# Another explicit order for the parts of the first stage of a three-stage kernel on one core

## The chip, the cores and the metric

One core of one Trainium2 chip runs the whole kernel. The metric is device time in microseconds (us) of one execution; lower is better. Times are given as the median of three timed runs, and one further execution was recorded by the hardware profiler. In the rows, PE is TensorE's matmul queue and PEld its weight loads, DVE is VectorE, ACT is ScalarE, POOL is GpSimd and SP is SyncE, which here only issues DMAs. A letter q behind an engine's name means its sequencer, which waits, branches and issues DMAs while the engine stays idle. TensorE's clock has two levels in the rows, 2.4 and 1.2 GHz; the granted clock is given as a share of 2.4 GHz.

## What is computed

Three layers follow each other. The inputs are float32, and only the output of the last layer leaves the chip.

```python
def _attn_ref(x, state):                      # x: 4 x 8 x 512 x 64, state: 4 x 8 x 32 x 64
    scores = scale * np.matmul(x, state.transpose(0, 1, 3, 2))
    a = softmax(scores)                       # over the 32 states
    xread = np.matmul(a, state)
    scores2 = scale * np.matmul(state, x.transpose(0, 1, 3, 2))
    a2 = softmax(scores2)                     # over the 512 tokens
    sread = np.matmul(a2, x)
    return np.concatenate([xread, sread], axis=2)

def _moe_ref(x, w_gate, w1, w2, capacity):    # 2176 rows of 512, 8 experts, top 1
    logits = x @ w_gate
    expert_idx = np.argmax(logits, axis=1)
    # each row goes to its expert, in order, while the expert has room
    h = np.maximum(np.einsum('ecd,edf->ecf', disp, w1), 0.0)
    y = np.einsum('ecf,efd->ecd', h, w2)
    out[i] = gate_w[i] * y[expert_idx[i], pos[i]]

def _moe2_ref(x, w_in, w_out):
    h = x @ w_in
    return (h * np.clip(h + 3.0, 0.0, 6.0) / 6.0) @ w_out
```

## The kernel before, in words

The kernel is one function `full` with three stages. The first stage is `phase1`: attention for the four batches, the gate logits, the choice of an expert for each row, the place of each row in its expert's list, and the tables from which the second stage reads its trips. Towards its end the first expert tile (256 rows) is worked too. The second stage goes through the other expert tiles, and the third multiplies all rows with `w_in` and `w_out`.

**What sets the order.** `phase1` is written as some 150 named parts, most of them Python generators with a `yield` after an instruction or a few. The string `ORDER` lists the parts' names; each word runs its part to its next `yield` (`name*3` three times), and the tile framework is told to keep that order. So `ORDER` is a hand-written interleaving: an engine gets its instructions in the order in which the words make them, and executes its queue strictly in that order. A second constant, `ALT`, says which engine does some of the parts' operations.

```python
        going = {}
        for n, k in ((w.split("*") + [1])[0:2] for w in ORDER.split()):
            for _ in range(int(k)):
                if n not in going:
                    f, *a = parts.pop(n)
                    going[n] = f(*a) or iter(())
                next(going[n], None)
```

**The parts**, with batch b and half f (four heads each) as digits, `soft_max10` being batch 1, half 0:
- `tr` transposes the input tiles on TensorE (L276) and ScalarE copies them out (L278); `scores` multiplies (L284) into the PSUM tile `pss`. `soft_max` takes the row maximum from `pss` on VectorE (L294), `soft_exp` the exponential from `pss` on ScalarE (L300), and `turn` transposes `pss` in blocks on VectorE (L303). So `pss` is read by two engines.
- `read_max` reduces on VectorE (L311) and subtracts on GpSimd (L313, two operands in SBUF); `read_exp` is on ScalarE (L316); `read_sum` reduces on VectorE (L320 to L324) and multiplies on GpSimd (L326, two operands in SBUF) or, where `ALT` says so, on VectorE; `read_turn` is VectorE's (L329).
- `e2_turn` (L337, L339), `s_read` (L354), `s_scale` (L360 and four DMAs, L364), `s_turn` (L369, L372) and `s_logits` (L378, L380, L383 and a DMA, L386) make the 32 state rows of a batch and their logits. `read` with a batch and an index 0 to 7 multiplies (L400) and copies out (L403 VectorE, L405 ScalarE). `rows_out` (L409) stores the batch's rows to `x_rows` in DRAM (L412).
- `count` (L419 to L434), `total` (L439, L441), `first_expert` (L446 to L471), `sums` (L477, L478), `place` (L485 to L507), `before` (L513 to L517) and `lists` (L532 to L538) are chains of small VectorE instructions with some on GpSimd and ScalarE; `lists2` multiplies one-hot tiles (L544) and adds them to the list of rows `LT` (L547 for batch 0, L549 for the others). `tables` and `halves` (L665 to L781) make the trip tables on VectorE.
- `raws` loads the first expert's weights; `w00` to `w13` split each of the eight pieces into two parts: a cast on ScalarE (L824) and a subtraction of two SBUF operands (L826) on VectorE or GpSimd.
- `early` stores an empty row to `x_rows` by DMA (L617), and GpSimd writes into the source tile behind it (L618). `e_rows` casts the first row numbers (L951) and gathers 256 rows on GpSimd's queue (L858); `e_x` transposes them (L846, L849, L851), `e_m` is the first product of the first expert tile (96 matmuls at L903, L907, L909), `e_y` the second (96 matmuls at L921, L931), with the result stored at L937.

One PSUM tile, `bank`, holds many of the small results (`s_read`, `s_turn`, `s_logits`, `sums`, `lists2` and others write parts of it, and ScalarE and VectorE read them).

**Behind the first stage** GpSimd reads the table (L1347), casts row numbers from `LT` (L1133) and gathers the next tiles' rows (L858), TensorE transposes them (L846), and SP issues, in this order, the store of the first tile's result (L937), two loads of second-layer weights (L1080, L1082) and the next expert's weights (L814).

Of the kernel before, what the change touches and what calls it, by code (L numbers as in the profile page):

```python
# [32 lines left out]
    tr11 setup2*2 tr10 setup1 tr11 setup2 soft_exp01 read_max01 prep_gate e2_turn00 scores10 read_sum00 consts tr12 e2_turn00 s_read00 setup2  # L33
    e2_turn01 tr12 read_sum00*2 tr13 s_read00 setup2 soft_max10 read_max01 e2_turn01 tr13 s_read00 scores11 turn10 read_exp01 read_sum00 soft_exp10
    tr20 read_max10 inputs setup2 tr20 setup2 read_turn00 setup2*2 setup3 setup2 read_init0 read_sum01*2 soft_max11 read_sum01 read_init1 s_read01
    setup2 s_scale0 read06 read04 read_max10 turn11 read_exp10 soft_exp11 s_scale0 read_max11 tr21 tr22 tr21 read_sum01 scores20 setup3 tr23 s_read10
    read_sum10 setup3 s_read10 consts setup2 tr22 read04 read_sum10 e2_turn10 read_sum10 tr23 setup3 read_turn01 read_max11 read00 read_sum10 read06
    s_turn0 setup3 scores21 soft_max20 read_exp11 turn20 s_ids0 read05 read_turn10 read00 read_max20 turn21 read05 setup3 s_turn0 setup3 read_max20
    read_sum11 read01 read07 read01 read02 e2_turn10 read07 read03 soft_max21 s_logits0 read02 read03 read_exp20 read_max21 rows_out0 s_logits0 early
    read_sum11 count0 rows_out0 read_sum20 count0 e2_turn11 read10*2 count0 s_logits0 tr30 read_sum20 setup3 s_read10 e2_turn11 read_max21 count0 tr31  # L40
    setup3 s_scale0 setup3 read_sum11 setup3 count0 consts before0 setup3 tr30 read14 read_sum11 first_expert soft_exp20 read_exp21 first_expert tr31
    read_sum20 consts before0 read12 first_expert s_scale1 e2_turn20 read_sum21 first_expert*2 scores30 read_turn11 first_expert setup3 count0
    s_read11 setup3 first_expert before0 read_sum21 soft_exp21 s_read20 tr32 first_expert read_sum21 read15 read14 first_expert*2 raws total0 read12
    s_scale1 e2_turn20 tr32 soft_max30 s_read20 sums0 read13 place0 raws place0 e2_turn21 turn30 place0 read_sum21 read_turn21 s_turn1 read_sum20
    read13 tr33 place0 read_max30 raws read15 first_expert place0 e2_turn21 read16 read_turn20 place0 tr33 total0 place0 raws read_max30 place0
    s_read20 soft_exp30 s_scale2 read_init2 read11 scores31 s_logits0 s_turn1 place0 read17 lists0 e2_turn30 s_read21 read11 lists0 read16 read17 w00
    read27 lists0 s_logits1 s_scale1 read_exp30 lists0 read24 lists0 read27 read25 lists0 rows_out1 s_scale2 turn31 soft_max31 lists0*2 s_ids2
    soft_exp31 s_logits1 read_max31 s_turn2 read26 read25 lists0 count1 lists0*3 read24 first_expert lists20 count1 read26 read_sum30 consts read23
    lists20 s_read30 count1 read_max31 read20 e_rows read_exp31 read_sum30 s_read30 e2_turn31 s_turn2 read23 e2_turn30 count1 read20 e_rows read_sum30
    read21 e2_turn31 count1 read_sum31 rows_out1 before1 read_sum30 s_read30 s_logits2 read_sum31 count1 w01 read_turn30 consts read22 read_init3  # L50
    read22 read34 read_sum31 w02 read21 read32 read_sum31 read32 s_ids1 read30 read34 s_logits2 total1 read_turn31 w00 s_read31 sums1 e_x0 w03 read31
    read30 w02 read33 s_scale3 read31 e_x0 read36 e_x1 e_x0 s_scale3 e_ok before1 s_turn3 place1 read35 read33 rows_out2 total1 read37 raws count2
    before1 count2 e_g s_turn3 w01 e_x1 s_logits1 read36 w03 s_logits1 e_x1 read37 s_logits3 read35 s_logits3 place1 count2 rows_out3 e_m0 count2
# [1570 lines left out]
```

## Time and profile before

| | us |
|---|---|
| median of three runs | 563.12 |
| lowest and highest | 562.98, 563.13 |
| the profiled execution, as timed | 564.15 |
| span of the profiled execution, first instruction to last | 562.4 |

The profiled execution is 1.0 us above the median, and 1.75 us of its time lie outside its span. In the profile, the timeline lists an engine's instructions with start, duration and, in square brackets, the idle time ahead of an instruction and what ended it; neighbours of one line are merged (x2). The table of stretches gives for each stretch the busy time of each engine in us and its instructions (x), TensorE's granted clock as a share, the DMA engines' share and their rate. The chain of work goes back from the last instruction, at each step to what released it.

### The profile page before, as it was taken

To read this page: it belongs to the slowest core of one execution; us is meant where nothing else is said; L and a number is where in the kernel's file an instruction comes from. 1 tells how busy PE (TensorE), PEld (TensorE's weight loads), DVE (VectorE), ACT (ScalarE), POOL (GpSimd) and SP (SyncE) were. 2 spreads that over 40 slices of the span, in tenths; PEclk is the share of its full clock that TensorE was granted. 3 is DMA by queue.
4 is the path that set the end of the run, shared out by engine and by line. 5 is a ranking of instruction groups with operands and counts; after the bars stand their busy time and mean duration, and the time that the engine had idled before them with its cause. 6 is when DMAs were issued, how large, how long until landed. Compare 5 with 4: busy or idle time off the path is not lost.

```text
span 562.4 us, 10121 instructions
## 1 busy us (share of the span) xinstructions
PE 532.6 (95%) x3772; PEld 466.5 (83%) x3772; DVE 309.0 (55%) x729; ACT 218.0 (39%) x461; POOL 144.5 (26%) x198
## 2 busy tenths in 40 slices
PE   5898899899999999999999999999999999999990
PEld 3566698796969898999998889999999998888880
DVE  3799978428735774676788953343334343222330
ACT  5577553225304250524444343333333343323340
POOL 1554645401610110117768732001001000000002
PEclk9798889999999999999999999999999999999997
DMA  6825730896989795336664312001001010000001
GB/s 136 184 103 218 247 111 20 281 401 232 374 283 401 251 377 174 98 113 226 224 209 148 115 37 76 1 23 53 1 19 58 1 31 19 20 0 1 0 13 57
DMA packets 52169, 74.99 MB, mean 133 GB/s; under 512 B 23089, under 2 KB 31537, under 8 KB 51602
## 3 DMA queue, kind: packets, MB, share of 16 engines
q1 hardware_dynamic: 49634, 66.83, 35.4%
q0 software_dynamic: 2208, 7.38, 3.9%
q8 instruction: 32, 0.52, 0.4%
q14 instruction: 23, 0.19, 0.1%
q10 hardware_dynamic: 272, 0.07, 0.1%
HBM read 70.62 MB, written 16.23 MB: 154 GB/s over the span
## 4 chain that ended last, share of the span: by engine, by line
issue 38%; PE 31%; DMA 15%; DVE 11%; ACT 3%; POOL 1%; POOLq 0%; SPq 0%; DVEq 0%; ACTq 0%
PE pm L921 8%; PE pm L903 7%; DMA out_dram<-o,fid 7%; DMA raw<-in_moe_w_dram 3%; DMA st<-in_moe_w_out_dram 3%; PE psX L400 2%; PE pm L1252 2%; PE p L1286 2%; PE pss L284 2%; PE pss L903 2%; DVE v L1096 1%; PE psx L276 1%; DVE g L1299 1%; DVE v L1094 1%; DVE v L1092 1%
## 5 line engine op out<-in xcount | busy, mean ns | idle before, releaser
L1286 PE MATMUL p<-yT,wh 128*128 128x256 f32 (+1 forms) x768 | 116.7, 294 | 0.0
L1286 PEld LDWEIGHTS p<-yT,wh 128*128 128x128 f32 x768 | 109.3, 188 | 7.8
L1299 DVE SCALAR_TENSOR_TENSOR g<-u,p 128x256 f32<-128x256 f32 x110 | 44.9, 409 | 111.0 <-ACT u L1298 110.9
L1298 ACT ACTIVATE u<-p,b 128x256 f32<-128x256 f32 x110 | 51.1, 464 | 103.4 <-PE p L1286 103.3
L1300 ACT CAST gh<-g 128x256 fp32r<-128x256 f32 x110 | 43.9, 399 | 79.9 <-DVE g L1299 79.9
L1464 POOL DMA_INDIRECT out_dram<-o,fid x14 | 14.0, 1000 | 215.9 <-ACT o L1463 190.8
L1286 PE MATMUL p<-yT,wl 128*128 128x256 f32 (+1 forms) x384 | 66.8, 296 | 0.9 <-POOL wl L1111 0.9
L1324 PE MATMUL po<-wh,gh 128*128 128x512 f32 x156 | 61.2, 392 | 0.0
L1324 PE MATMUL po<-wh,gl 128*128 128x512 f32 x156 | 61.2, 392 | 0.0
L1324 PE MATMUL po<-wl,gh 128*128 128x512 f32 x156 | 61.0, 391 | 0.0
L1286 PEld LDWEIGHTS p<-yT,wl 128*128 128x128 f32 x384 | 55.4, 189 | 2.6 <-POOL wl L1111 1.7
L1306 DVE TENSOR_TENSOR gl<-g,gh 128x256 fp32r<-128x256 f32 x84 | 34.4, 410 | 32.2 <-ACT gh L1300 32.2
L903 PE MATMUL pm<-xth,w1h 128*128 128x256 f32 x160 | 44.6, 283 | 1.8 <-ACT xth L849 1.5
L921 PE MATMUL pm<-hth,w2h 128*128 128x256 f32 x160 | 45.5, 284 | 0.0
L921 PE MATMUL pm<-hth,w2l 128*128 128x256 f32 x160 | 45.1, 282 | 0.0
L921 PE MATMUL pm<-htl,w2h 128*128 128x256 f32 x160 | 45.1, 282 | 0.0
L903 PE MATMUL pm<-xth,w1l 128*128 128x256 f32 x160 | 43.6, 277 | 0.0
L1111 POOL TENSOR_TENSOR wl<-v,wh 128x1024 fp32r<-128x1024 f32 x14 | 34.4, 2454 | 35.4 <-ACT wh L1110 35.0
L903 PE MATMUL pm<-xtl,w1h 128*128 128x256 f32 x160 | 41.6, 277 | 0.0
L1324 PEld LDWEIGHTS po<-wh,gl 128*128 128x128 f32 x156 | 29.3, 188 | 7.0 <-POOL gl L1306 0.6
L903 PEld LDWEIGHTS pm<-xth,w1h 128*128 128x128 f32 x160 | 30.1, 188 | 5.1 <-issue 2.9
L1306 POOL TENSOR_TENSOR gl<-g,gh 128x256 fp32r<-128x256 f32 x26 | 25.1, 967 | 30.6 <-ACT gh L1300 30.6
(307 smaller groups left out, 1029.1 us busy)
## 6 DMA issues: line engine op xcount, KB each, us to landing
raw<-in_moe_w_dram SPq DMA_DIRECT2D x80, 512.0 KB
st<-in_moe_w_in_dram SPq DMA_DIRECT2D x16, 512.0 KB
st<-in_moe_w_out_dram SPq DMA_DIRECT2D x16, 512.0 KB
x_rows<-xrow SPq DMA_DIRECT2D x4, 1072.0 KB
xb<-in_x_dram SPq DMA_DIRECT2D x32, 128.0 KB
yg<-y_pad SPq DMA_DIRECT2D x13, 258.0 KB
out_dram<-zt SPq DMA_DIRECT2D x2, 1536.0 KB
y_pad<-y SPq DMA_DIRECT2D x5, 516.0 KB
```

Source lines behind the costliest of these rows:

```text
L284: T.matmul(ps[64 * a:64 * a + 64, :], sT[:, 2 * b + f, 64 * a:64 * a + 64], st[b]["xT"][:, 2 * f + a], start=True, stop=True)
L400: T.matmul(ps, s["aT"][:, f, j, :], bd[:, 2 * b + f, :], start=True, stop=True)
L903: T.matmul(ps[:, j], W1[l][k][:, ls], xT[r][:, k], start=n == 0, stop=n == 11)
L921: T.matmul(ps[:, j], W2[l][k // 2][:, k % 2, ls], hT[k // 2][r][:, k % 2], start=k == 0 and i == 0, stop=k == 7 and i == 2)
L1111: (V if m in (0, 2) else G).tensor_tensor(out=wl, in0=v, in1=wh.bitcast(F32), op=ALU.subtract)
L1286: T.matmul(out, w[:, 128 * k:128 * k + 128], r(k), start=n == 0, stop=n == 11)
L1298: A.activation(out=u, in_=ps, func=AF.Relu, bias=b3)
L1299: V.scalar_tensor_tensor(out=g, in0=u, scalar=6.0, in1=ps, op0=ALU.min, op1=ALU.mult)
L1300: A.copy(gh[:, 0:w], g)
L1306: eng.tensor_tensor(out=gl, in0=g[:, 0:n], in1=gh[:, 0:n].bitcast(F32), op=ALU.subtract)
L1324: T.matmul(po[t], l[:, ls], r[:, 512:1024], start=m == 0 and i == 0, stop=m == 15 and i == 2)
L1464: G.indirect_dma_start(out=out, out_offset=bass.IndirectOffsetOnAxis(ap=fid[0:n, t:t + 1], axis=0), in_=o[0:n], in_offset=None, bounds_che ...
```

## The change

Only the string `ORDER` is replaced. Every part is run as often as before and makes the same instructions with the same operands on the same engines; `ALT` and all other code are the same. What differs is the order in which each engine's queue gets them. All 33 lines of the string differ; the first three and two later ones of each version stand here.

```diff
 ORDER = """
-    setup0 inputs setup0*4 tr00 prep_state0 tr01 tr00 setup2 setup3 prep_state0*2 tr01 scores00 setup2 tr02 setup3 setup2 setup0 tr03 setup2 setup0
-    setup1 tr02 prep_state2 setup2*2 tr03 setup1*2 inputs*2 prep_state2 setup2*2 inputs prep_state2 soft_max00 prep_state2 scores01 prep_state2 tr10
-    prep_state2 setup3*2 prep_gate soft_exp00 setup2 zeros turn00 read_max00 setup2*2 read_max00 setup2*2 read_exp00 soft_max01 turn01 setup2 setup3
...
-    read21 e2_turn31 count1 read_sum31 rows_out1 before1 read_sum30 s_read30 s_logits2 read_sum31 count1 w01 read_turn30 consts read22 read_init3
-    read22 read34 read_sum31 w02 read21 read32 read_sum31 read32 s_ids1 read30 read34 s_logits2 total1 read_turn31 w00 s_read31 sums1 e_x0 w03 read31
...
+    setup0 inputs setup0 inputs setup0 tr00 setup0 setup2 setup0 tr00 setup2 prep_state0*2 setup0 tr01 setup2 prep_state0 tr01 setup2 setup0 setup2
+    scores00 tr03 setup2 setup1 tr03 tr02 setup3 prep_state2 setup2 tr02 zeros setup2 soft_max00 turn00 inputs tr10 scores01 setup2*2 setup1
+    read_max00 setup2 setup3 read_max00 soft_exp00 tr11 setup2 tr10 turn01 prep_state2 setup3 setup2 read_exp00 prep_state2 inputs read_max01 tr11
...
+    w02 w00 read_turn31 sums1 s_read31 read21 s_read30 read23 before1 read_sum30 w01 before1 w02 consts s_ids1 s_scale1 raws read37 w01 read21 read37
+    s_read30 read31*2 e_x0 read33 read35 e_x1 read_turn30 s_scale3 read30 s_scale3 s_logits2 w03 place1 s_logits1 e_x0 read33 read35 read30 raws
...
 """
```

Counting the words through gives each engine's queue. VectorE has 272 instructions in the first stage, GpSimd 109, ScalarE 123, SP 71 DMAs. The positions in those queues (from 0) that the next part speaks of:

| instruction | queue | before | after |
|---|---|---|---|
| `soft_max00` L294, `turn00` L303 | VectorE | 8, 11 | 9, 10 |
| second half of `bd` memset L164 against the second copy of `sT` L253 | VectorE | 5, after it | 4, ahead of it |
| `turn01` L303, `soft_max01` L294 | VectorE | 14, 13 | 13, 15 |
| `read_sum10` L320 | VectorE | 34 | 34 |
| `count0` L422, `total1` L439 | VectorE | 52, 127 | 55, 121 |
| `lists20` L547, `e_rows` L951 | VectorE | 109, 112 | 118, 120 |
| `w00`, `w02` L826 | VectorE | 129, 130 | 123, 129 |
| `e_x0`, `e_x1` L851 | VectorE | 132, 142 | 137, 138 |
| `s_logits3` L380 | VectorE | 144 | 147 |
| `halves` L718 | VectorE | 206 | 199 |
| last `LT` addition L549 | VectorE | 261 | 258 |
| `early` memset L618, first `lists0` L538 | GpSimd | 53, 70 | 68, 69 |
| gathers of `e_rows` L858 | GpSimd | 78, 79 | 76, 77 |
| `w01`, `w03`, `w11` L826 | GpSimd | 84, 86, 102 | 82, 84, 101 |
| `early` store L617 | SP | 37 | 44, behind two of the `raws` |

For the first score tile `soft_exp00` stands ahead of `turn00` before, and behind it after; for the other seven `turn` stands ahead of `soft_exp` in both. On TensorE `scores01` stands ahead of `tr10` before and behind it after, and the third transposes' parts `tr02` and `tr03` change places.

## Rows read from the trace of the kernel before

**Rows 1.** Table of stretches (length; PE, PEld, DVE, ACT, POOL busy; clock; DMA).

```profile
28.50:53.10 24.60, 23.04 (x251) 15.62 (x249) 22.96 (x76) 19.33 (x52) 12.07 (x32) 1.00 0.49 183
67.50:73.20 5.70, 5.70 (x28) 5.69 (x27) 5.57 (x33) 1.82 (x4) 3.00 (x6) 0.50 1.00 368
80.00:90.00 10.00, 9.23 (x77) 8.87 (x75) 9.65 (x40) 4.76 (x8) 5.71 (x5) 1.00 0.00 0
```

**Rows 2.** Chain that ended last, behind the first stage: start, length, what.

```profile
95.52 3.53 DMA xg<-x_rows,col
101.39 0.39 SPq L937
147.56 11.51 PE pm L921 x96
```

**Rows 3.** VectorE's timeline, instructions long and short: start, length, what, idle before.

```profile
36.02 0.73 DVE L422 TENSOR_TENSOR d<-L,m 128x40 f32<-128x40 f32 x1
50.65 1.85 DVE L536 TENSOR_SCALAR ol<-io,lo,idmi 32x128 fp32r<-32x128 f32 x1
57.81 2.64 DVE L439 TENSOR_TENSOR Gs<-Gs,O 128x8 f32<-128x8 f32 x1
61.00 4.47 DVE L826 TENSOR_TENSOR w1l<-raw,w1h 128x1024 fp32r<-128x1024 f32 x2
70.36 0.16 DVE L439 TENSOR_TENSOR Gs<-Gs,O 128x8 f32<-128x8 f32 x1
71.92 1.22 DVE L826 TENSOR_TENSOR w2l<-raw,w2h 128x1024 fp32r<-128x1024 f32 x1
80.80 0.33 DVE L536 TENSOR_SCALAR ol<-io,lo,idmi 32x128 fp32r<-32x128 f32 x1
82.34 1.78 DVE L718 SCALAR_TENSOR_TENSOR Q<-Q,c 128x8 f32<-128x8 f32 x1
```

**Rows 4.** GpSimd's timeline, five lines.

```profile
54.58 1.28 POOL L858 DMA_INDIRECT xb<-x_rows,ecol  x1 [2.16 <-PE psX L400]
56.15 1.00 POOL L858 DMA_INDIRECT xb<-x_rows,ecol  x1 [0.30 <-issue]
58.07 2.35 POOL L826 TENSOR_TENSOR w1l<-raw,w1h 128x1024 fp32r<-128x1024 f32 x1
60.98 3.42 POOL L826 TENSOR_TENSOR w1l<-raw,w1h 128x1024 fp32r<-128x1024 f32 x1 [0.42 <-ACT w1h L824]
81.71 2.38 POOL L826 TENSOR_TENSOR w2l<-raw,w2h 128x1024 fp32r<-128x1024 f32 x1 [7.08 <-ACT w2h L824]
```

**Rows 5.** VectorE's timeline, the start and the list's way to the gather.

```profile
13.98 0.72 DVE L303 STREAM_TRANSPOSE R<-pss 128x512 f32<-128x512 f32 x1 [3.12 <-ACT e L300]
20.83 0.69 DVE L294 TENSOR_REDUCE m<-pss 128x1 f32<-128x512 f32 x1 [1.39 <-PE pss L284]
28.48 0.67 DVE L320 TENSOR_REDUCE rs<-R 128x16 f32<-128x512 f32 x1
53.13 0.29 DVE L547 COPY LT<-bank 128x144 f32<-128x144 f32 x1
94.07 0.30 DVE L549 TENSOR_TENSOR LT<-LT,bank 128x144 f32<-128x144 f32 x1
```

**Rows 6.** TensorE's timeline, six lines.

```profile
13.29 0.63 PE L276 MATMUL psx<-identk,xb 128*128 128x128 f32 x4 [1.01 <-DMA xb<-in_x_dram]
52.65 0.30 PE L544 MATMUL bank<-oh,ol 32*128 32x144 f32 x1 [1.56 <-DVE d L422]
65.87 0.71 PE L400 MATMUL psX<-bd,aT 128*128 128x264 f32 x2 [2.09 <-DVE xrow L403]
67.51 0.58 PE L903 MATMUL pss<-xT,w1h 128*128 128x256 f32 x1
98.35 0.28 PE L921 MATMUL pss<-xb,w2l 128*128 128x256 f32 x1
100.50 0.66 PE L846 MATMUL pxt<-identk,xg 128*128 128x128 f32 x4 [0.68 <-DMA xg<-x_rows,col]
```

More of the change, by code (lines that the diff above doesn't have):

```diff
@@ L34 @@
[L34 to L49, printed above, removed]
@@ L58 @@
-    e_g*2 e_m3 e_m2 e_m3 raws halves consts e_m2 tables e_ok s_logits3 w11 place3 halves s_scale3 lists1 place3 e_m3 lists21 tables halves tables
-    place2 e_m3 halves w13 lists2 place2 halves w11 w13 e_y1 lists2*5 s_scale2 e_ok tables halves lists21 e_y1 lists2 halves e_y0 place3 lists2 halves
-    lists2*2 tables halves lists2 tables e_y0*3 halves lists2 e_y0 tables halves place3 lists22 lists3*2 halves*2 lists3 tables lists3 e_g halves
-    lists3*2 e_y0 s_logits2 lists3 halves lists3 e_y1 lists22 e_y0 s_logits3 lists3*2 halves*2 lists3*2 tables halves lists3 e_g halves tables*2
@@ new lines @@
+    place0 e2_turn20 e2_turn21 place0 read17 read_max30 place0 s_turn1 e2_turn20 s_read20 place0 soft_exp30 e2_turn21 read_max30 read15 scores31
+    place0 read17 place0 read_turn21 s_read20 read_exp30 w00 place0 turn31 raws lists0 place0 read_init2 place0 read_max31 read14 read13 early lists0
+    read15 s_read20 read_sum30 read22 read_max31 s_logits0 lists0 s_read21 soft_max31 read14 s_logits1 read27 lists0 read13 read24 s_logits1 rows_out1
+    lists0*2 read22 count1 read_sum30 lists0 consts read26 s_scale2*2 lists0 e2_turn30 total0 count1 lists0 s_turn2 read_exp31 count1 soft_exp31
@@ new lines @@
+    place1 e_x0 s_turn3 e_x1 w03 e_x1 read34 read36 read32 rows_out2 s_turn3 place1 read32 count2 e_ok read36 read34 e_m0 e_m1 e_m0 s_logits3
+    rows_out3 s_ids2 count2 e_m0*2 place1 e_m1 count2 s_logits3 total1 count2 w10 e_m0 count3*2 place1 w12 e_m0 count2 place1 count3 count2 count3*2
+    place1 total2 e_m1 e_m0 w10 place1 before3 sums2 e_m1 count3 total2 e_m1 before2 place1 lists1 before2 raws e_m1 lists1 before3 total3 e_g e_m0
+    place2 e_m1 e_m2 total3 lists1*2 s_logits2 e_m2 e_ok lists1 totals first_expert e_m2 w12 s_scale2 e_g e_m1 e_m2 rows_out2 before3 before2 e_m3
@@ new lines @@
+    tables lists1 place2 raws consts e_m2 tables e_m2 place2 e_g lists1 e_m2 tables lists1*2 tables*2 lists1*3 tables e_g tables e_m3 tables halves
+    lists1 e_m3 tables place2 w11 halves e_m3*2 tables place2 s_logits2 s_logits1 e_m3 tables lists21 e_m3 sums3 place2 w13 e_m2 tables e_ok s_scale3
+    e_m3 place3 s_logits3 e_y1 lists21 place2 w11 w13 place2 lists2 halves place3 e_y0 place2 place3 halves place3 e_y0 tables e_y1 lists2*3 s_ids3
+    place3 tables lists2*2 place3 e_y1 place3 e_y0 halves e_y0 lists2*4 tables e_y0 lists2*2 lists22 tables e_y1 halves place3 lists3*2 e_g halves
@@ L63 @@
+    place3 halves lists3*3 halves e_g tables e_g e_ok rows_out3 lists3 halves lists3*3 halves lists22 lists3 e_y1 halves e_g halves lists3*3 halves*2
+    e_y0 lists23 halves lists23 halves*2 e_gt e_y0 halves e_y1 halves e_y1 halves e_gt e_y0 halves s_logits3 halves*3 e_y0 e_y1*3 halves
 """
```

22 lines of the change are left out of this document (14 added, 8 removed).

## The prediction

> **What bounds the kernel now.** I read four views in this order. The page gives TensorE 95% of the span, which hides that the first 100 us have other limits. So I went to the chain that ended last, to see what the second stage hangs on. There, GpSimd's gather of the next rows starts at 95.52 and takes 3.53 us to land, and SP's store of the first tile's result goes at 101.39 [rows 2]. The weight loads follow in SP's queue; from there to the end I find only work that hangs on those loads or on TensorE. From 80 to 90 us DMA moves nothing at all [rows 1], so an earlier start of the loads meets no other transfer. I take it that a us won ahead of the second gather's transposes (100.50 [rows 6]) is a us won at the end.
>
> The gather needs the last addition to the row list `LT`, at 94.07 [rows 5]. TensorE's last matmul of the first tile starts at 98.35 and ends at 98.63, 1.87 us ahead of the transposes at 100.50 [rows 6]. So the row list is the bound, and the first tile's products are 1.87 us behind it as the next one.
>
> The table of stretches tells what the row list waits for. From 28.5 to 53.1 VectorE is busy 22.96 of 24.60 us and TensorE 23.04 [rows 1]: both are full, ScalarE (19.33) and GpSimd (12.07) are not. From 67.5 to 73.2 VectorE is full, and TensorE runs at half clock (0.50).
>
> The timeline of VectorE shows that part of this fullness is no work. An instruction on 8 columns (L439) takes 0.16 us at 70.36 and 2.64 us at 57.81. Two weight splits (L826) take 4.47 us, where one alone takes 1.22 [rows 3]. At 58.07 to 60.42 and 60.98 to 64.40 GpSimd runs its own splits, of two operands in SBUF [rows 4]: VectorE's instruction ends when GpSimd's does. The surplus of the five long rows is L422 0.57 (against the 0.16 row), L536 1.52 (1.85 less 0.33), L439 2.48, L826 2.03 (4.47 less twice 1.22) and L718 1.62: 8.2 us [rows 3].
>
> **The change part by part.** No instruction is added or removed, so I follow four stretches of the path and ask how much later or earlier each ends.
>
> *Start to 28.48 (first L320 of batch 1).* VectorE's first L303 waits 3.12 us for ScalarE's exponential of the same PSUM tile [rows 5]. In the new queue L303 stands straight behind L294 and the exponential comes after it: VectorE's wait goes. What is late next is the second score tile: `scores01` now stands behind `tr10`, whose transposes wait for input until 13.29 [rows 6]. The memset L164, moved ahead of the second copy of `sT`, delays the first scores a little. Later VectorE waits 1.39 us more for TensorE at 20.83 [rows 5], which an earlier exponential could shorten too. So: at least 0.7 (13.98 less 13.29, if all hangs on the input), at most 4.5 (3.12 and 1.39). I take 3.1, as the wait itself is the nearest row.
>
> The Trainium skill (PSUM — Partial Sum Buffer, section PSUM bank collisions raise a hardware error) says that the hardware doesn't arbitrate between two engines at one bank, and that the program has to keep them apart, reads included. By that the wait can't vanish: it moves to ScalarE, which waits 0.72 us for the L303 row. If ScalarE were on the path this term would be 2.4 and the whole sum 7.6; ScalarE's 5.3 idle us of 24.6 [rows 1] speak for the full term.
>
> *28.48 to the first copy of the list (L547, 53.13).* That is 24.65 us. VectorE idles 1.64 in it [rows 1] and loses 0.57 and 1.52 to GpSimd [rows 3]; 20.9 us are work. In the new queue GpSimd's L313 of batch 2 stands beside reductions and PSUM reads of VectorE, and that of batch 3 beside L320 and L294, so I take both losses as gone. L547 is nine places later (118 against 109, while L320 is 34 in both), small instructions of 0.16 at most or big ones that leave later stretches: 0.9. I keep the idle time at 1.64. That makes 23.4, a gain of 1.2. More than 1.6 is not to be had, as TensorE has only 24.60 less 23.04 to give. The lower bound is a loss of 2: two waits of GpSimd are new here. Its first `lists0` operation stands behind the memset of `early`, which waits for a small store that is now queued on SP behind two weight pieces of 512 KB. All of `lists0`, and VectorE's copy of the list, are behind that.
>
> *List copy to the first matmul of the first tile.* Now 53.13 to 67.51 [rows 5, 6], 14.4 us, because VectorE's and GpSimd's splits hold each other up ahead of `e_x`. In the new order: the first gather starts 1.45 us after the copy, the second 1.57 later [rows 4], landing takes 3.53 [rows 2], the transposes 0.63 (the L276 row [rows 6]), ScalarE's cast about the same: 7.8 us. VectorE has done both its splits by then (places 123 and 129; `e_x` is 137), and runs PSUM reads while GpSimd does its two. GpSimd's gathers end at 4.0, four small operations follow, and two splits of 2.35 end at about 9.4; the ninth matmul needs them. I take 9.4. If the splits take 3.42, as one does where it meets VectorE's [rows 4], it is 11.5 and more: 11.8. If the first eight matmuls cover the wait, 8.0. So a gain of 5.0, between 2.6 and 6.4.
>
> *First matmul to the second gather's transposes.* 67.51 to 100.50, 33.0 us. GpSimd's split `w11` (2.38 [rows 4]) still runs beside VectorE's tables and split `w13`, so I let the 1.62 of L718 stand as lost. New is that VectorE's copy of the last logits (L380, place 147, ahead of `count3` and all that follows) stands behind twelve of the first matmuls, the last four of which wait for the fourth weight piece: about 1 us. So a loss of 1.0, between a loss of 3 (both splits of W2 meeting VectorE's tables, at 1.62 to 2.03 each) and a gain of 1.6 (L718's surplus gone, no new wait).
>
> The sum is 3.1 + 1.2 + 5.0 - 1.0 = 8.3 us. The profiled execution took 564.15, 1.0 above the median; it would take 555.85. Against the median, 563.12 less 8.3 is **554.8 us**. The bounds add up to a loss of 1.7 and a gain of 14.1; both ends at once in four stretches is unlikely, and the forecast's own range is 550 to 559.
>
> **The rivals.**
>
> *The start's lead is lost to TensorE.* TensorE is as full as VectorE up to 53.1 [rows 1], and its input decides until 13.29. Then the first stretch gives 0.7, the second nothing, the third 5.0, the fourth -1.0: 4.7, or 558.4 us. For it: a full TensorE. Against: the new queue gives it the transposes earlier.
>
> *The order doesn't do what it says.* GpSimd's splits start when the gather has been issued and ScalarE's cast is done, not when the list says. If VectorE comes to its small two-operand instructions (place 139 on) while the second split runs, it waits to the split's end, as at 57.81. Then the third stretch gives 2.6, and the fourth loses 2.35 more than taken: 3.1 + 1.2 + 2.6 - 3.35 = 3.6, or 559.5 us. The Trainium skill (SBUF — State Buffer, Who interferes with whom) has it that whichever of the two engines starts first holds the shared port pair for its whole instruction, and that issue order decides who blocks. The trace agrees at 57.81 to 60.45.
>
> *TensorE at 1.2 GHz: slower.* From 67.5 to 73.2 TensorE's 28 matmuls took 0.204 us each (5.70 by 28) at clock 0.50 [rows 1], against 0.120 later (11.51 for 96 [rows 2]). Ahead of that it had stood 2.09 us before 65.87 [rows 6]. In the new order it waits for the gather, the fourth piece, `w11` and the one-hot tiles, and could stay low. Of the tile's 192 matmuls some 165 ran at full clock before; all of them low cost 165 x 0.084 = 13.9 us. Of that 8.3 are paid by the lead and 1.87 by the slack: 3.7 slower, 566.8 us. It turns slower from 121 low ones on. Against it: in the stretch from 80 to 90 the clock was 1.00 [rows 1] although TensorE stood still there too (9.23 of 10 us busy).
>
> *Nothing is left.* New waits eat the lead, or the second stage's loads give it back: 563.
>
> **How the numbers follow.** The forecast (550 to 559) gets 0.57, the lost lead 0.13, the order that misses 0.10, nothing left 0.06, the slow clock and its like 0.14. A measurement of this kernel can tell about 0.2% (1.1 us) from no change. Faster is the first three, 0.80; same 0.06; slower 0.14. The range reaches from 549.5 to 562.0: it takes in the first three with the wide ends of their terms, and leaves out 0.20.
>
> **What would show it.** Right: the first L303 of VectorE at about 11 instead of 13.98; the list copy L547 at about 49; L439 at 0.16 and both splits of VectorE near 1.22; the first matmul at L903 near 58; the last L549 at about 86 and the transposes at 92. Wrong: a VectorE instruction of over 1 us on a few columns between GpSimd's two splits; GpSimd's first L538 waiting for a store; the granted clock near 0.5 after the first ten us of L903; the last L921 ending behind the gather. If the transposes come 8 us earlier and the end does not, my 1:1 step is wrong.

## The result, and the profile after

| | before | after |
|---|---|---|
| median, us | 563.12 | 556.51 |
| lowest and highest, us | 562.98, 565.73 | 554.55, 556.75 |
| profiled execution, us | 564.15 | 556.75 |
| its span, us | 562.4 | 554.9 |

Each median is of four runs; a fourth run of the kernel after, in a slower state of the chip at 563.84 us, counts in its median (556.27 without it) but not in the row of lowest and highest or in the ratio. The ratio is 0.9866, with an interval of 0.9843 to 0.9889; by the medians it is 6.6 us. Timed again on another chip (`after_again` below), the ratio was 0.9897 (0.9878 to 0.9916), 5.6 us by the medians. I take the change to be worth 5.6 to 6.6 us.

VectorE's timeline of the kernel after (start, length, what, and in brackets the idle time ahead and what ended it), for the rows of [rows 3] and [rows 5]:

```profile
10.61 0.71 DVE L303 STREAM_TRANSPOSE R<-pss 128x512 f32<-128x512 f32 x1
24.85 0.67 DVE L320 TENSOR_REDUCE rs<-R 128x16 f32<-128x512 f32 x1
48.45 0.30 DVE L547 COPY LT<-bank 128x144 f32<-128x144 f32 x1
48.87 0.16 DVE L439 TENSOR_TENSOR Gs<-Gs,O 128x8 f32<-128x8 f32 x1
49.56 1.22 DVE L826 TENSOR_TENSOR w1l<-raw,w1h 128x1024 fp32r<-128x1024 f32 x1
52.10 1.22 DVE L826 TENSOR_TENSOR w1l<-raw,w1h 128x1024 fp32r<-128x1024 f32 x1
72.96 0.16 DVE L718 SCALAR_TENSOR_TENSOR Q<-Q,c 128x8 f32<-128x8 f32 x1
73.22 2.35 DVE L494 TENSOR_TENSOR t<-t,O 128x40 f32<-128x40 f32 x1
86.06 0.30 DVE L549 TENSOR_TENSOR LT<-LT,bank 128x144 f32<-128x144 f32 x1 [0.34 <-PE bank L544]
```

The first L303 no longer waits, L439 and the two W1 splits have their plain lengths, and the list copy comes 4.7 us earlier, the last addition to the list 8.0. One new victim stands there: L494, 0.2 us elsewhere, takes 2.35. GpSimd's timeline shows its partner (73.10), and something the prediction did not have:

```profile
42.89 0.09 POOL L618 MEMSET zt<- 1x1 f32 x1 [3.79 <-DMA x_rows<-zt]
49.86 2.07 POOL L858 DMA_INDIRECT xb<-x_rows,ecol  x1 [2.85 <-PE psX L400]
52.23 1.96 POOL L858 DMA_INDIRECT xb<-x_rows,ecol  x1 [0.30 <-issue]
54.75 2.34 POOL L826 TENSOR_TENSOR w1l<-raw,w1h 128x1024 fp32r<-128x1024 f32 x1
57.19 2.33 POOL L826 TENSOR_TENSOR w1l<-raw,w1h 128x1024 fp32r<-128x1024 f32 x1
73.10 2.42 POOL L826 TENSOR_TENSOR w2l<-raw,w2h 128x1024 fp32r<-128x1024 f32 x1 [3.47 <-ACT w2h L824]
```

Both splits are clean now (2.34 and 2.33, where [rows 4] has 3.42), but the two gathers of the first rows take 2.07 and 1.96 us to issue, against 1.28 and 1.00 in [rows 4]. TensorE's timeline, for [rows 6]:

```profile
58.27 0.63 PE L846 MATMUL psc<-identk,xb 128*128 128x128 f32 x4 [1.18 <-DMA xb<-x_rows,ecol]
60.44 0.47 PE L903 MATMUL pss<-xT,w1h 128*128 128x256 f32 x1
92.57 0.66 PE L846 MATMUL pxt<-identk,xg 128*128 128x128 f32 x4 [0.85 <-DMA xg<-x_rows,col]
94.45 0.36 PE L903 MATMUL pm<-xth,w1h 128*128 128x256 f32 x1 [1.23 <-POOL col L1192]
```

So the lead over the kernel before is 3.63 us at L320, 4.68 at the list copy, 7.07 at the first L903 and 7.93 at the second gather's transposes. The span is 7.5 shorter. Where the last piece of the lead goes, the tables of stretches of the second stage's first product (its first L903 to its first L921) show; first before, then after (columns: length; PE, PEld, DVE, ACT, POOL busy; clock; DMA):

```profile
102.69:115.23 12.54, 12.54 (x111) 12.54 (x111) 6.04 (x16) 3.42 (x8) 2.55 (x4) 1.00 0.98 332
```

```profile
94.45:108.51 14.06, 14.06 (x110) 14.06 (x111) 5.42 (x15) 3.41 (x8) 3.22 (x4) 0.88 0.99 355
96.00:98.00 2.00, 2.00 (x11) 2.00 (x11) 0.23 (x2) 0.00 (x0) 0.03 (x1) 0.50 1.00 366
```

The same product takes 1.5 us longer, because TensorE runs at 1.2 GHz (0.50) for some 3.4 us of it. Its first L921 comes at 108.51 instead of 115.23: of a lead of 8.24 at the first L903 (102.69 to 94.45), 6.72 is left.

### The profile page after: what moved, and what is told of

Its sections match the earlier page's. It is cut to its first block, busy times and chain, and to the rows that moved or that the text cites. A ratio compares the mean times of both kernels' runs of the same rounds, so it can differ in the third digit from the quotient of the medians.

```text
span 554.9 us, 10128 instructions
## 1 busy us (share of the span) xinstructions
PE 527.0 (95%) x3772; PEld 463.7 (84%) x3772; DVE 302.7 (55%) x729; ACT 217.7 (39%) x461; POOL 141.9 (26%) x198
## 2 busy tenths in 40 slices
DMA packets 52169, 74.99 MB, mean 135 GB/s; under 512 B 23089, under 2 KB 31537, under 8 KB 51602
## 4 chain that ended last, share of the span: by engine, by line
PE 37%; issue 37%; DMA 10%; DVE 10%; ACT 3%; POOL 1%; SPq 1%; POOLq 0%; DVEq 0%; ACTq 0%
PE pm L921 10%; PE pm L903 10%; DMA out_dram<-o,fid 5%; PE p L1286 3%; PE po L1324 3%; PE pm L1252 2%; PE pm L1226 2%; PE psx L276 2%; DVE v L1096 1%; DVE g L1299 1%; PE pss L284 1%; DVE v L1094 1%; PE psX L400 1%; DMA st<-in_moe_w_in_dram 1%; DMA st<-in_moe_w_out_dram 1%
## 5 line engine op out<-in xcount | busy, mean ns | idle before, releaser
L903 PE MATMUL pm<-xth,w1h 128*128 128x256 f32 x160 | 45.1, 286 | 1.2 <-POOL col L1192 1.2
L921 PE MATMUL pm<-hth,w2h 128*128 128x256 f32 x160 | 45.5, 284 | 0.0
L921 PE MATMUL pm<-hth,w2l 128*128 128x256 f32 x160 | 45.1, 282 | 0.0
L921 PE MATMUL pm<-htl,w2h 128*128 128x256 f32 x160 | 45.1, 282 | 0.0
L903 PE MATMUL pm<-xth,w1l 128*128 128x256 f32 x160 | 44.1, 280 | 0.0
L903 PE MATMUL pm<-xtl,w1h 128*128 128x256 f32 x160 | 42.6, 283 | 0.0
L903 PEld LDWEIGHTS pm<-xth,w1h 128*128 128x128 f32 x160 | 30.6, 191 | 4.3 <-issue 3.5
```

The costliest lines, as they stand in the source:

```text
L903: T.matmul(ps[:, j], W1[l][k][:, ls], xT[r][:, k], start=n == 0, stop=n == 11)
L921: T.matmul(ps[:, j], W2[l][k // 2][:, k % 2, ls], hT[k // 2][r][:, k % 2], start=k == 0 and i == 0, stop=k == 7 and i == 2)
```

## The experiments

My theory after these traces: the lead is the sum of single waits taken away ahead of the second gather, and reaches the end but for what TensorE's clock takes back. The rivals: the gain sits in one place alone (the clock of the first tile's matmuls, or the splits that no longer meet); the gathers are long because of DMA traffic and not because of VectorE. A ratio is against the kernel before on the same chip, with its interval. A trace is of one execution: over nine executions with the order of the changed kernel up to the list copy, the copy lay between 47.2 and 49.1, so I don't read differences below 1 us between single traces.

| kernel | median, us | ratio | list copy | first L903 | 2nd transposes | first product of the 2nd stage, clock |
|---|---|---|---|---|---|---|
| before | 563.12 | 1 | 53.13 | 67.51 | 100.50 | 12.54, 1.00 |
| after | 556.51 | 0.9866 | 48.45 | 60.44 | 92.57 | 14.06, 0.88 |
| `after_again` | 557.79 | 0.9897 | 47.22 | 59.24 | 91.42 | 15.03, 0.84 |
| `turn_first` | 558.87 | 0.9907 | 48.56 | 62.74 | 94.55 | 14.37, 0.88 |
| `exp_first` | 559.75 | 0.9926 | 50.17 | 62.31 | 95.81 | 15.38, 0.82 |
| `swap_splits` | 557.68 | 0.9889 | 48.25 | 62.53 | 92.78 | 14.37, 0.88 |
| `splits_late` | 556.26 | 0.9849 | 47.69 | 57.30 | 91.48 | 15.52, 0.81 |
| `w11_vec` | 554.86 | 0.9847 | 47.73 | 59.38 | 90.50 | 14.04, 0.88 |
| `after_fill` | 556.70 | 0.9876 | 47.54 | 58.97 | 92.91 | 12.84, 1.00 |
| `w11_fill` | 554.14 | 0.9839 | 49.11 | 61.14 | 92.38 | 12.84, 1.00 |
| `late_fill` | 556.52 | 0.9872 | 47.73 | 57.38 | 93.69 | 12.84, 1.00 |
| `late_w11` | 556.59 | 0.9868 | 47.47 | 56.76 | 91.51 | 15.05, 0.81 |
| `front_only` | 557.67 | 0.9889 | 48.52 | 63.02 | 95.36 | 14.37, 0.88 |
| `back_only` | 567.36 | 1.0058 | 53.64 | 69.12 | 102.56 | 14.37, 0.88 |

**The two halves apart.** The order of one kernel up to the list copy, then that of the other, without the words already used:

```diff
 ORDER: front_only = the changed order up to and with the second lists20, then the order before
 ORDER: back_only  = the order before up to and with the second lists20, then the changed order
```

> The order of the changed kernel up to the list copy L547, and from there the order of the kernel before (words already used are left out). Theory (leads add up and pass 1:1 to the end): the list copy at about 48.5 us as in the changed kernel, a lead of 4.7; then 14.4 us to the first L903 as before, at about 63; the second gather's transposes at about 96, and a time of 558.4, a ratio of 0.992. Rival (the start's lead is lost, the gain sits in the clock of the first tile's matmuls and in the splits that no longer meet): L903 at about 66 to 67, the clock in the first six us behind it 0.5 as before, and 562 to 563 us.

> The other half: the order of the kernel before up to the list copy L547, and the order of the changed kernel behind it. Theory: the list copy at 53.1 as before, then 12.0 us to the first L903 (65.1) and 32.1 to the transposes (97.3), a lead of 3.2, a time of about 559.9 and a ratio of 0.994. The splits of VectorE take 1.22 and the gathers of the first rows about 2.0 each, as in the changed kernel. Rival (the gain sits here alone): 556.5 to 557.5. The two halves' gains should add up to that of the change (6.6 us).

`front_only` took 557.67 us, ratio 0.9889 (0.9870 to 0.9908). Its list copy came at 48.52 and its first L903 at 63.02, as the theory had it, though the clock behind it was still low, as the rival had it. In time the first half alone is already as good as the whole change, within the intervals.

`back_only` was slower than before: 567.36 us, 1.0058 (1.0036 to 1.0080). Neither case had that. VectorE's timeline shows why:

```profile
53.64 0.31 DVE L547 COPY LT<-bank 128x144 f32<-128x144 f32 x1 [1.22 <-PE bank L544]
56.06 0.69 DVE L320 TENSOR_REDUCE rs<-R 128x16 f32<-128x512 f32 x1 [0.98 <-ACT R L316]
57.16 0.10 DVE L951 CAST ecol<-LT 128x2 uint32<-128x2 f32 x1
```

The cast of the row numbers (L951) follows the copy by 3.5 us, against 0.4 in [rows 5]'s kernel and in the kernel after: the cut leaves work of batch 3 undone that the changed order has ahead of L951, and VectorE's strict queue takes it first. So this run is no test of the second half; it shows that the gather's start hangs on that one place in VectorE's queue. I went on with single moves.

**The exponential and L303.** One word, first put back in the changed order, then put forward in the order before:

```diff
 exp_first, from the kernel after
-    ... zeros setup2 soft_max00 turn00 inputs tr10 ... read_max00 soft_exp00 tr11 ...
+    ... zeros setup2 soft_max00 soft_exp00 turn00 inputs tr10 ... read_max00 tr11 ...
 turn_first, from the kernel before
-    prep_state2 setup3*2 prep_gate soft_exp00 setup2 zeros turn00 read_max00 ...
+    prep_state2 setup3*2 prep_gate turn00 soft_exp00 setup2 zeros read_max00 ...
```

> The changed kernel with one word moved: ScalarE's exponential of the first score tile stands ahead of VectorE's first L303 again. Theory: the wait of about 3 us ahead of that L303 comes back (start near 14), the first L320 of batch 1 moves from 24.85 to about 28, and the end by as much: 559.6 us, 3.1 above the changed kernel. Rival (the input decides, as in the 0.7 bound): L320 near 25.5 and at most 557.2.

> The kernel before with one word moved: VectorE's first L303 stands ahead of ScalarE's exponential of the first score tile. Theory after the run that put the exponential first again in the changed order: the swap alone frees VectorE of its wait of 3.1 us, but the first L320 of batch 1 comes only about 1 us earlier (27.5 instead of 28.48), because TensorE's wait for ScalarE's copy of xT at 17.74 and the low clock behind it (0.50 from 16 to past 19 us) stay: about 562 us, ratio 0.998. Rival (the prediction's reading, the wait itself is the term): L320 at about 25.4, and 560 us, ratio 0.9945.

`exp_first` took 559.75 us, 0.9926 (0.9907 to 0.9945): the expected loss in time, but L320 came at 25.90, only 1.05 later than in the kernel after. I concluded that the wait is worth 1 us at L320 and that `turn_first` would give about that. It gave 5.0 us: 558.87, 0.9907 (0.9891 to 0.9924). That theory fell, and the rival, the prediction's own reading, was nearer, though it too expected less. The gain doesn't sit in the splits or in the first tile's clock alone either: in `turn_first` the splits still meet (6.75 us), and the clock is still low in the first tile. VectorE's timeline of `turn_first`:

```profile
10.72 0.70 DVE L303 STREAM_TRANSPOSE R<-pss 128x512 f32<-128x512 f32 x1
25.12 0.67 DVE L320 TENSOR_REDUCE rs<-R 128x16 f32<-128x512 f32 x1
48.56 0.31 DVE L547 COPY LT<-bank 128x144 f32<-128x144 f32 x1 [0.25 <-PE bank L544]
54.00 6.75 DVE L826 TENSOR_TENSOR w1l<-raw,w1h 128x1024 fp32r<-128x1024 f32 x2
```

One word moves L320 by 3.36 us and the list copy by 4.57, as much as the whole new order (3.63 and 4.68). The kernel before shows how the wait of 3.12 us spreads, on ScalarE and then on TensorE:

```profile
16.58 0.63 ACT L316 ACTIVATE R<-R 128x512 f32<-128x512 f32 x1 [2.63 <-POOL R L313]
```

```profile
17.74 1.11 PE L337 MATMUL psc<-identk,e 128*128 128x128 f32 x4 [2.20 <-ACT xT L278]
```

L303 comes late, so L311 and GpSimd's L313 come late, and ScalarE stands 2.63 us at L316. The copies of `xT` (L278) are behind it in its queue, so TensorE stands 2.20 us, and its clock is 0.50 from about 15.5, where that wait begins, to past 22 us. In `turn_first` little of it is left. TensorE from 10.0 to 28.5, in the kernel before, in `turn_first` and in `exp_first`:

```profile
10.00:28.50 18.50, 15.29 (x162) 9.79 (x161) 12.08 (x27) 12.53 (x29) 8.62 (x30) 0.82 0.76 171
```

```profile
10.00:28.50 18.50, 17.77 (x182) 11.38 (x181) 15.94 (x34) 14.57 (x34) 10.03 (x35) 1.00 0.76 172
```

```profile
10.00:28.50 18.50, 16.35 (x175) 10.31 (x173) 15.01 (x31) 13.77 (x33) 8.64 (x27) 1.00 0.76 171
```

This is where the two runs part. In `exp_first` VectorE's first L303 waits again (2.14 us, to 13.09) and TensorE is less busy, but the clock stays at 1.00, and only 1.05 us are lost at L320. The traces show the wait and the low clock together in `before` and `back_only`; why the wait alone didn't bring the clock down in `exp_first` stays open.

**Splits beside the gather.** VectorE's two W1 splits moved behind both L851 of the first rows:

```diff
 splits_late, from the kernel after
-    w02 w00 read_turn31 ... before1 w02 consts ... e_x1 w03 e_x1 read34 ...
+    w02 read_turn31 ... before1 consts ... e_x1 w03 e_x1 w00 w02 read34 ...
```

> The changed kernel with VectorE's two splits of W1 moved behind both L851 of the first rows, so that none runs beside GpSimd's two gathers. Theory (while VectorE runs a split, GpSimd's gather doesn't get on): the gathers take 1.0 to 1.3 us each instead of 2.07 and 1.96, the second transposes come at about 56.5 instead of 58.27, the first L903 at about 59 instead of 60.44, and the time falls by about 1 us to 555.5. Rival (traffic of the DMA queues makes the gathers long): they stay near 2.0, the splits then end behind the first rows, L903 goes on only at about 62, and the time is 1 to 2 us longer than that of the changed kernel.

GpSimd's timeline, then two lines of TensorE's, then two windows of its clock:

```profile
49.11 1.28 POOL L858 DMA_INDIRECT xb<-x_rows,ecol  x1 [1.73 <-PE psX L400]
50.69 1.00 POOL L858 DMA_INDIRECT xb<-x_rows,ecol  x1 [0.30 <-issue]
```

```profile
57.30 0.47 PE L903 MATMUL pss<-xT,w1h 128*128 128x256 f32 x1
59.03 0.39 PE L903 MATMUL pss<-xT,w1l 128*128 128x256 f32 x1 [1.25 <-DVE w1l L826]
```

```profile
58.00:60.00 2.00, 0.50 (x2) 0.30 (x2) 2.00 (x2) 1.58 (x4) 0.00 (x0) 1.00 0.71 261
62.00:64.00 2.00, 2.00 (x10) 2.00 (x11) 1.93 (x15) 0.00 (x0) 0.47 (x1) 0.50 0.63 244
```

The gathers are back at 1.28 and 1.00. In the kernel after, the first split ends at 50.78 and the gather's issue 1.15 later, the second at 53.32 and the issue 0.87 later: each begins when the split is over. The moved splits also free the weight buffers later, so that the next loads go at 54.63 instead of 50.80; but around the first gather DMA is nearly idle in both, as the tables show, first of the kernel after and then of this one:

```profile
49.00:51.00 2.00, 2.00 (x18) 1.50 (x17) 2.00 (x4) 1.93 (x6) 1.14 (x1) 1.00 0.10 22
```

```profile
48.30:50.30 2.00, 2.00 (x18) 1.53 (x16) 1.97 (x6) 1.82 (x6) 1.19 (x1) 1.00 0.10 25
```

So for the first gather the traffic is ruled out, and it is VectorE's split that held it. For the landing of the second gather the two causes are not told apart. From the list copy to the first L903 it is now 9.6 us, against 12.0 in both traces of the changed kernel (11.4 to 12.0 with `after_fill`, `w11_fill` and `w11_vec`).

The time is 556.26 us, 0.9849 (0.9822 to 0.9876), within the interval of the changed kernel's first timing and just below that of its second. Its lead of 3.1 us over the kernel after at the first L903 is lost in the first product: 1.25 us go to the split that now comes late, and then the clock falls to 0.50, after TensorE was busy only 0.50 us from 58 to 60. It fell in the profiled execution; by the mean clock of each, two of the six executions had 0.990 and 0.991 and took 553.71 and 552.97 us, four had 0.982 and took 556.18 to 557.67.

**The swap and the splits' place alone.** To the order of `turn_first`:

```diff
 swap_splits, from turn_first
-    ... count1 read20 e_rows read_sum30 ... rows_out1 before1 read_sum30 ...
+    ... count1 read20 e_rows w00 w02 read_sum30 ... rows_out1 before1 w02 read_sum30 ...
 (and the same words taken out further down)
```

> The kernel before with two things moved: VectorE's first L303 ahead of the exponential (turn_first), and VectorE's two splits of W1 to where the changed order has them, right behind the cast of the row numbers, so that they no longer meet GpSimd's splits. Theory (these two places carry the change): the gathers take about 2.0 us each because the splits run beside them, GpSimd's splits 2.35, VectorE's 1.22 instead of 5.61 and 6.75, the first L903 comes at 60.5 instead of 62.74, and the time is 2 us below that of turn_first: about 556.7, ratio 0.987, that of the whole change. Rival (the splits were hidden behind the gather anyway): 558.9 as turn_first.

It took 557.68 us, 0.9889 (0.9867 to 0.9911), 1 us below `turn_first` by ratio, which the intervals don't tell apart. The steps were wrong in part. GpSimd's and VectorE's timelines:

```profile
50.19 1.62 POOL L858 DMA_INDIRECT xb<-x_rows,ecol  x1 [1.11 <-PE psX L400]
52.11 1.91 POOL L858 DMA_INDIRECT xb<-x_rows,ecol  x1 [0.30 <-issue]
54.58 2.34 POOL L826 TENSOR_TENSOR w1l<-raw,w1h 128x1024 fp32r<-128x1024 f32 x1
```

```profile
54.90 2.57 DVE L326 TENSOR_TENSOR R<-R,rs 128x512 f32<-128x512 f32 x1
```

The gathers are held, as expected. But with the splits out of the way the next two-operand instruction meets GpSimd's split: L326, 0.69 us in the kernel after, takes 2.57. The first L903 comes at 62.53, not at 60.5. So for an earlier L903 moving the splits isn't enough; what else stands on VectorE beside GpSimd's splits has to be moved as well, and the changed order does that. The time doesn't need it: 557.68 us is the whole change's time on the same chip (557.79), and the second transposes come at 92.78, as in the kernel after (92.57). Behind the first L903 the first product runs at full clock here, where `turn_first` had it low; first `turn_first`, then `swap_splits`:

```profile
62.74:76.58 13.84, 13.84 (x106) 13.84 (x106) 12.32 (x65) 7.51 (x15) 5.33 (x15) 0.89 0.66 254
```

```profile
62.53:74.78 12.25, 12.25 (x108) 12.25 (x106) 12.11 (x65) 7.39 (x15) 5.32 (x15) 1.00 0.66 248
```

So in time the theory that these two places carry the change came out, within the intervals, but not by the steps that it named.

**w11 on VectorE.**

```diff
-    rd31 rd37 sub30 wp01 wp03 wp11
+    rd31 rd37 sub30 wp01 wp03
```

> The changed kernel with the split w11 on VectorE instead of GpSimd. Theory: VectorE's L494 at 73.22 takes 0.19 us instead of 2.35, the split costs VectorE 1.22, so the last addition to the list and the end come 0.9 us earlier: ratio 0.985 against the kernel before. Rival (L494 only waits in a stretch that isn't on the path, or the second product of the first tile waits for w11): same as the changed kernel, or up to 1.2 us slower.

```profile
72.20 0.19 DVE L494 TENSOR_TENSOR t<-t,O 128x40 f32<-128x40 f32 x1
74.27 2.35 DVE L826 TENSOR_TENSOR w2l<-raw,w2h 128x1024 fp32r<-128x1024 f32 x2
```

As the theory had it, in VectorE's timeline: L494 is 0.19, and the split is paid with 1.2 us (two in 2.35). From the list copy to the last addition to the list it is 36.1 us, against 37.6 and 37.7 in the two traces of the changed kernel. The time is 554.86 us, ratio 0.9847 (0.9828 to 0.9866), as forecast; the interval meets that of the changed kernel's first timing and lies clear of that of its second.

**TensorE's idle stretch filled.** 19 matmuls of the identity around the second gather's transposes, whose output is overwritten or never read; alone, and with w11 on VectorE. The two other pairings, of `splits_late` with these matmuls and the first L903 repeated 14 times, and of `splits_late` with `w11_vec`, stand with them:

```diff
 after_fill, w11_fill, late_fill
+    def fill(ps, n):
+        for _ in range(n):
+            T.matmul(ps[:, 0:128], ident, ident, start=True, stop=True)
...
+            ps = p3.tile([128, 512], F32, name="pxt", tag="3")
+            if first:
+                fill(ps, (7, 5)[t])
```

> The changed kernel with 19 more matmuls of the identity on TensorE, ahead of the second gather's transposes (7), between them (5) and behind them (7), where it stands idle from 89.9 to 94.5 us; what they write is overwritten. Theory (the idle stretch is what brings the clock of 0.50 from 95.5 to 98.8): the clock stays at 1.00 there, the first matmuls of the second stage take 0.12 us each instead of 0.21, and the time falls by 1.5 to 2 us. Rival (the clock falls anyway, or the loads of the weights bind behind it): no change within 0.2%, or 0.5 us slower if the added matmuls stand in the way of the transposes.

> The changed kernel with w11 on VectorE and, in TensorE's idle stretches around the second gather's transposes, the 19 matmuls of the identity. In w11_vec the second stage's first product took 14.04 us (92.28 to 106.32), 1.5 more than the 12.54 of the kernel before, at a clock of 0.61 and 0.54 from 92 to 96; from the first L921 of the second stage to the end every trace so far has 446 to 447 us. Theory (the idle stretch brings the low clock, and the low clock takes back what the lead gives): the clock stays at 1.00 from 88 to 106, that product takes 12.6 to 12.9 us, the first L921 of the second stage comes at about 105.2, and the time is 1 us below that of w11_vec: about 553.8, ratio 0.983. Rival (the clock isn't what takes it back, or the fills delay the transposes by as much): L921 at 106.3 or later and a ratio of 0.9847 or above.

> The kernel with VectorE's two W1 splits behind the gathers (splits_late), and in it TensorE's idle stretches filled: its first matmul of the first tile is repeated 14 times while it waits for the splits, and the 19 matmuls of the identity stand around the second gather's transposes. Theory (splits_late lost its 3.1 us of lead at the first L903 to the clock of 0.50 from 61 to 65 and again from 93 to 99): both stretches run at 1.00, the lead stays, and the time is 3 to 5 us below that of splits_late: about 552, ratio 0.978. Rival (the lead is lost to the splits' wait of 1.25 us and to other waits): 555 to 556.

> The changed kernel with both single improvements: VectorE's W1 splits behind the gathers (splits_late), and the split w11 on VectorE (w11_vec). Theory: gathers of 1.0 to 1.3 us, first L903 at about 57.4, no L494 of 2.35 us; the last addition to the list at about 83 and 553.5 us, ratio 0.982, if the clock stays up in the first tile, and 555 if it falls to 0.50 at about 60 as in splits_late. Rival (ScalarE's casts of W2, which stand behind the first products, set the end of the first tile): no better than w11_vec, 0.9847.

The second stage's first product in `after_fill`, with a window of the first tile, and in `w11_fill`:

```profile
94.83:107.67 12.84, 12.84 (x113) 12.84 (x112) 5.58 (x15) 3.41 (x8) 3.20 (x4) 1.00 1.02 379
76.00:80.00 4.00, 4.00 (x23) 4.00 (x23) 3.86 (x21) 1.68 (x4) 2.05 (x4) 0.57 0.00 0
```

```profile
94.30:107.14 12.84, 12.84 (x114) 12.84 (x112) 5.33 (x15) 3.42 (x8) 3.15 (x4) 1.00 1.02 380
```

Where the idle stretch is filled, the clock stays at 1.00 and the product takes 12.84 us; where it isn't, ten traces have 14.04 to 15.52 at a low clock (`back_only`, without a lead, among them), and only the kernel before has 12.54. So the idle stretch is what brings the low clock in these kernels; why it didn't in the kernel before is not shown. But the time of `after_fill` doesn't fall: 556.70 us, 0.9876 (0.9857 to 0.9895). In this execution the clock was low from 76 to 80 instead, behind the 3.4 us from the last L903 of the first tile to its first L921 (71.56 to 74.99), of which TensorE waits 1.73 us for VectorE's L909 behind the long L494. That stretch is as long in both traces of the changed kernel, where the clock stayed up behind it; why it fell here stays open. `w11_fill`, where it is 1.6 us without a wait, took 554.14 us, 0.9839 (0.9811 to 0.9867): the lowest of all, but within the interval of `w11_vec`. So that the fills save time at the end is not shown.

`late_fill` took 556.52 us, 0.9872 (0.9845 to 0.9900), and `late_w11` 556.59, 0.9868 (0.9844 to 0.9892); in both about the rival's time came out. In `late_fill` the first L903 is at 57.38 and the clock stays at 1.00 behind it, but the second product starts at 75.83: it waits for L909, which stands behind an L494 of 2.36 us beside w11, and w11 starts only when ScalarE's cast of it ends at 72.39. In `late_w11` there is no such L494, and the first L903 is at 56.76, but the clock is 0.50 from about 61 to 64 and the last L903 comes at 73.27, later than in `w11_vec` (71.97); the rival had named ScalarE's casts for that. The earlier gather brought nothing in either.

**The changed kernel once more.**

> The changed kernel itself once more, beside the two kernels below on one chip. Expected: the ratio of before, 0.987, within its interval; in its trace the list copy at 47.5 to 48.5, the gathers at about 2.0 us each, L494 at 2.35 us, and a stretch of clock 0.50 either about 76 to 80 or about 95 to 99.

557.79 us, 0.9897 (0.9878 to 0.9916), above the expected 0.987 and its interval; the trace is nearly as expected (list copy at 47.22, gathers 2.07 and 1.96, L494 2.35), with a clock of 0.50 from 92 to 98.

## Why the prediction was right, and where it wasn't

The time of 556.5 us lies in the range and in the forecast's own range, 1.7 above the predicted 554.8. That it came so near is luck in part: the third step was 2.6 us too large and the fourth 1.9 too small. Step by step:

*Start to L320: predicted 3.1, measured 3.63 (3.36 from the one word alone).* Right in size and place, and the mechanism is shown by `turn_first`: the wait is gone and nothing as late takes its place. The bound of 0.7 by the second score tile didn't decide. Nor did the wait move to ScalarE (2.4): the exponential comes behind ScalarE's copies anyway, at 12.38 in the kernel after and at 14.36 in `turn_first`, and waits for no L303 (which ends at 11.32 and 11.42). What the prediction missed is that the wait in [rows 5] also led to TensorE's wait, with a low clock to past 22 us, and that this one swap gives 5.0 us in the order before. Taken out of the changed order it costs only 1.6 to 3.4 us (0.9926 against 0.9897 and 0.9866), so the steps' gains don't simply add up.

*L320 to the list copy: predicted 1.2, measured 1.05.* The size is right by luck. Both losses are gone as predicted (L422 takes 0.20, L536 0.33), but in this execution a wait takes half of it back. ScalarE's first cast of the weights waits for its piece, and TensorE and VectorE wait behind it:

```profile
42.78 1.04 ACT L824 CAST w1h<-raw 128x1024 fp32r<-128x1024 f32 x1 [1.27 <-DMA raw<-in_moe_w_dram]
44.16 0.71 PE L400 MATMUL psX<-bd,aT 128*128 128x264 f32 x2 [1.04 <-ACT xrow L405]
45.70 0.15 DVE L380 COPY L<-bank 32x8 f32<-32x8 f32 x1 [1.11 <-PE bank L378]
```

`front_only` has the same wait (1.54); the seven other traces with this order up to the list copy have at most 0.22 of it and take 22.5 to 22.7 us, a gain of 1.9 to 2.2. That is above the 1.6 that TensorE was said to have to give. Nor do the losses need new places: `turn_first` has a gain of 1.21 with GpSimd's instructions where they were in the queue; there L536 is back at 0.33 although nothing was moved away from it, only shifted in time, and L422 still takes 0.73. The feared wait for the `early` store came (3.79 us on GpSimd, to 42.89), but VectorE's `hi` (L507), which the next instruction needs as well, ends at 42.81, so it cost 0.2 us at most.

*List copy to the first L903: predicted 5.0, measured 2.39.* This is the term that failed, just outside its bounds of 2.6 to 6.4 (2.35 to 2.95 over the five traces with this order). The step said that the gathers end 4.0 us after the copy and the two GpSimd splits decide at 9.4. The gathers ended at 5.7, because VectorE's own splits, now placed beside them, held each up; the landing took 3.95 us from there, against 2.4 in [rows 2] (3.53 less 1.10 of issue), which stays open between the loads at that time and the gather itself; and ScalarE had one copy of a result ahead of the cast. The gather decided, at 12.0. `splits_late` and `late_w11`, with the gathers free, had 9.6 and 9.3: the 9.4 was right for a gather that nothing holds.

*First L903 to the second transposes: predicted a loss of 1.0, measured a gain of 0.86.* L718's surplus of 1.62 is gone, but L494 lost 2.16 in its place, as the prediction let stand; `w11_vec` gives back 1.5 of it. The gain is put down to the clock, which these traces support without separating it: [rows 1] had 28 matmuls at half clock, 5.70 us instead of some 3.4, and the changed kernel has the whole first product at 1.00 (60.44 to 73.03, 12.6 us against 15.1); `turn_first` and `swap_splits` above differ by 1.6 us in that product, and by as much in this whole step. The prediction saw the clock only as a risk.

*1:1 to the end: 7.93 at the transposes, 7.5 in the span, 6.6 by the medians.* Nearly right, for a reason that the prediction didn't have. From the first L921 of the second stage to the end all traces read have 446.2 to 447.2 us, so from there it is 1:1 within 1 us (447.2 is the kernel before, which gives 0.8 back). But on the way there the low clock takes 1.5 us (2.5 in `after_again`, which led by 9.1 at the transposes). The rival of the slow clock had the right mechanism in the wrong place: in the first tile the clock got better, and it struck one tile later, and only in part.

The rival that the order misses came half true: a VectorE instruction of over 2 us on a few columns was there (L494), with w11 and not between GpSimd's first two splits. Its reading of the row at 57.81, that the engine which starts first holds on, isn't what that row shows (below).

## What to carry to other kernels

When VectorE waits for another engine at one PSUM tile, follow the chain behind the wait before pricing it: here 3.1 us on VectorE were also ScalarE's and TensorE's wait and TensorE's clock, and one word gave 5.0 us where a whole new order gave 5.6 to 6.6. Two-operand work of VectorE in SBUF holds up GpSimd's gathers and is held up by its arithmetic, and whatever is moved away from such a meeting leaves its place to the next instruction in the queue; clearing the gathers alone brought no clearly shorter time here. A lead can be paid back in part at TensorE's clock; look at the granted clock behind each idle stretch before counting a lead 1:1. And read a step in more than one trace: the same order took 22.5 to 24.0 us in one step, by whether a transfer had landed.

## What the runs showed of the hardware

**A gather's issue on GpSimd stands still while VectorE runs a subtraction of two SBUF operands.** 2.07 and 1.96 us beside splits of 1.22, 1.28 and 1.00 without. The Trainium skill (SBUF — State Buffer, section Who interferes with whom) has it that a VectorE instruction with two SBUF inputs contends with a GpSimd instruction that reads SBUF, but reports that `tensor_tensor` did not stall a DMA issued from GpSimd's queue, and infers that descriptor generation needs the write side. Here it did stall; these gathers take their row numbers from SBUF, which may be the difference, but no run here separates it.

**The engine that waits doesn't get in between.** In `turn_first` VectorE's two splits took 6.75 us, beside these on GpSimd:

```profile
53.72 2.36 POOL L826 TENSOR_TENSOR w1l<-raw,w1h 128x1024 fp32r<-128x1024 f32 x1
56.04 0.18 POOL L383 COPY xsc<-L 32x8 f32<-32x8 f32 x1
56.19 2.34 POOL L826 TENSOR_TENSOR w1l<-raw,w1h 128x1024 fp32r<-128x1024 f32 x1
```

VectorE's pair started at 54.00 and ended at 60.75. Two splits take 2.35 us where nothing holds them (74.27 above), so at that rate nothing was done before about 58.4, when the second of GpSimd's was ending, although a small copy lay between them. In the kernel before, L439 started at 57.81, 0.26 us ahead of GpSimd's split at 58.07 [rows 3, 4] and beside two small copies of GpSimd's that lead up to it (57.80 and 57.93), and was held to the split's end all the same; so starting first, as the prediction read that row, is not what let GpSimd through there.

**TensorE's clock and idle stretches.** TensorE was busy 0.63 and 0.66 us in the two stretches of 2 us ahead of the low clock of the kernel after (90 to 94). In the kernel before it was busy 1.26 and 0.66 us ahead of the same product (98 to 102), and the clock stayed at 1.00; in `after_again` it was busy 0.79 and 1.21 us (88 to 92), and the clock was at 0.50 from about 91.4. What decides is not shown. The Trainium skill (TensorE: Matmul & The Clock Gate, section HAM oscillation — how this bites in real kernels) describes such a start at low clock behind a wait for a DMA; in the second stage the traces without the fills agree, but for that of the kernel before. In the first tile the same stretch of 3.4 us, of which TensorE waits 1.7 to 1.8, was followed by the low clock in four executions (`after_fill`, `late_fill`, `exp_first`, `back_only`) and not in the two of the changed kernel, and that stays open.
